# Attention and a three-way max feed-forward layer on one core: immediate biases, an earlier first load, a reordered start, and 12 matmuls on constants

## Chip, core and metric

The kernel runs on one core of a Trainium2 chip. The metric is the device time in microseconds (us) of one execution. Engines: TensorE (PE, with its weight loads PEld), VectorE (DVE), ScalarE (ACT), GpSimd (POOL), and SyncE (SP), which issues DMAs.

## The reference

```python
# q, k, v: (8 batches, 12 heads, 448, 64), fp32
scores = q @ k^T / sqrt(64)
e      = exp(scores - m)                    # m: maximum of the row
attn   = e / (sum(e) + exp(-m) + 1e-9)      # softmax with one more 1 in the sum
x      = (attn @ v) as (3584 tokens, 768)
h      = max(x @ w1, x @ w2, x @ w3)
out    = h @ w_out
```

## The kernel before

The 12 heads of a batch are three groups of four heads, so there are 24 groups. All arithmetic on TensorE is in fp16. A group's K and Q are transposed, scores are computed with keys on partitions, ScalarE takes the exponential, a matmul with ones gives the denominators, and ScalarE makes their reciprocals as exp(-ln(d)). Groups 0 to 2 (batch 0) run in a hand-written start, cut in two parts by queries, among feed-forward pieces for batch 0. From group 4 on a loop does one group per pass. Groups 0 to 4 are transposed on TensorE, later ones by a DMA transpose issued one or two passes ahead; group 5's is queued at the end of the start (`X5`).

```python
def load_group(i, which="qkv"):            # GpSimd queue, casts to fp16 in the DMA
    ... tile(..., tag="ld_" + name, bufs=6 if name == "v" else 5)
    for hp in range(2): load_half(nc.gpsimd, tiles[name], name, i, hp)

first = {}                                 # group 0: K on SP's queue, Q on ACT's, both fp32
for name, eng in (("k", nc.sync), ("q", nc.scalar)):
    ... for hp in range(2): load_half(eng, first[name], name, 0, hp)
load_group(1, "kq"); make_identity(nc, ident16); load_group(0, "v"); ...
one_b, e_b, ln_lam = ...                   # [128, 1] biases in SBUF, read through pointers
load_weight(0); load_weight(1); load_group(3, "kq"); load_weight(2)
load_group(4, "kq"); load_group(3, "v"); load_group(5, "kq"); ...
# (cut)
ops = {"C": pair_qk, "T": pe_transpose_both, "S": scores_part (three units),
       "s": scores_part (the last unit), "A": av_part (denominators, ln, exp, numerators),
       "M": moe, "U"/"V"/"W": visit_a/b/c, "E": sums, "X": transpose_later, "F": flush}
start = """
    C0 T0 S00 T1 s00 S10 T2 s10 A00 S20 A10 s20 S01 A20 s01
    S11 M1 s11 M1 M1 A01 S21 M1 s21 M1 T3 M1 A11 U3 M1 A21 V3 T4 E30 M1 M1 W3 E31 X5 F
"""
# (cut)
for i in range(4, 24):
    load_group(i + 3)
    visit_a(i); av_group(i - 2) (or feed-forward for i < 5); visit_b(i); ...; moe(gap)
    if i + 1 < PE_TR: pe_transpose_both(i + 1)      # PE_TR = 5
    flush(); visit_c(i); den_group(i - 1)
    transpose_later(i + 2); ...; moe(gap); flush()
```

`T3` is the transpose of group 3, `M1` one feed-forward piece, `W3` the third score visit of group 3, which ends the start.

The softmax here doesn't subtract the row's maximum and nothing guards it: scores larger than these inputs give would overflow.

Of the kernel before, what the change touches and what calls it, by code (L numbers as in the profile page):

```python
# [10 lines left out]
FP32 = mybir.dt.float32  # L11
# [3 lines left out]
ts = bass.ts  # L15
# [3 lines left out]
EDIV = 8.0  # L19
# [3 lines left out]
def kernel(  # L23
# [69 lines left out]
    def load_group(i, which="qkv"):  # L93
        tiles = raw.setdefault(i, {})
        for name in which:
            tiles[name] = ld_pool.tile(
                [128, 2, NJ, D], MMDT, tag="ld_" + name, name="ld_" + name, bufs=6 if name == "v" else 5
            )
            for hp in range(2):
                load_half(nc.gpsimd, tiles[name], name, i, hp)  # L100

    first = {}
    for name, eng in (("k", nc.sync), ("q", nc.scalar)):
        first[name] = cpool.tile([128, 2, NJ, D], FP32, name="first_" + name)
        for hp in range(2):
            load_half(eng, first[name], name, 0, hp)
    load_group(1, "kq")
    ident16 = cpool.tile([128, 128], MMDT, name="ident16")
    make_identity(nc, ident16)
    load_group(0, "v")  # L110
# [5 lines left out]
    one_b = cpool.tile([128, 1], FP32, name="one_b")  # L116
    nc.vector.memset(one_b, 1.0 / EDIV)
    e_b = cpool.tile([128, 1], FP32, name="e_b")
    nc.vector.memset(e_b, -math.log(EDIV))
    ln_lam = cpool.tile([128, 1], FP32, name="ln_lam")  # L120
    nc.vector.memset(ln_lam, math.log(LAMBDA))

# [19 lines left out]
    def copy_qk(i, n):  # L142
        st = state.setdefault(i, {})
        if n == 0:
            st["qk16"] = p16_pool.tile([128, 2, NJ, 2, D], MMDT, tag="qk16", name="qk16")
        src = first["kq"[n]] if i == 0 else raw[i]["kq"[n]]
        nc.vector.tensor_copy(
            out=st["qk16"][:, n].rearrange("p j s d -> p s j d"), in_=src
        )

    def pair_qk(i):
        for n in range(2):
            copy_qk(i, n)

    def pe_transpose(i, n):
        st = state.setdefault(i, {})
        if n == 0:
            st["qkT"] = att_pool.tile([128, 2, NJ, 128], MMDT, tag="qkT", name="qkT")
        trT = ps1.tile([128, NJ, 128], MMDT, tag="bank1", name="trT")
        for j in range(NJ):  # L160
            if i == 0:
                nc.tensor.transpose(
                    out=trT[:, j, :], in_=st["qk16"][:, n, j].rearrange("p s d -> p (s d)"),
                    identity=ident16,
                )
                continue
            for s in range(2):
                nc.tensor.transpose(  # L168
                    out=trT[s * KC : s * KC + KC, j, :], in_=raw[i]["kq"[n]][:, s, j], identity=ident16
                )  # L170
        nc.vector.tensor_copy(  # L171
            out=st["qkT"][:, n].rearrange("p j c -> p (j c)"),
            in_=trT.rearrange("p j c -> p (j c)"),
        )
# [31 lines left out]
    def scores_visit(i, units):  # L206
# [8 lines left out]
        for j, stp in stps:  # L215
            nc.scalar.activation(  # L216
                out=st["eT"][:, j], in_=stp[:, :, 0:S], func=AF.Exp, scale=scale, bias=e_b
            )
# [27 lines left out]
    def den_group(i):  # L246
# [10 lines left out]
        nc.scalar.activation(out=lnd, in_=dps[:, :, 0:S], func=AF.Ln, bias=one_b)  # L257
        st["rb"] = small.tile([128, 2, S], FP32, tag="rb", name="rb")
        nc.scalar.activation(out=st["rb"], in_=lnd, func=AF.Exp, bias=ln_lam, scale=-1.0)  # L259
# [24 lines left out]
    def scores_part(i, part, last=False):  # L284
# [3 lines left out]
        if not last:  # L288
            st["eT", part] = e_pool.tile([128, NJ, 2, nq], MMDT, tag="eT", name="eTp")
        eT = st["eT", part]  # L290
        for j0 in (6,) if last else (0, 2, 4):
            n = min(2, NJ - j0)
            stp = ps2.tile([128, 2, 512], FP32, tag="bank2", name="stp")
            for jj in range(n):
                score_tile(st["qkT"], stp[:, :, ts(jj, nq)], j0 + jj, q0, q1)
            nc.scalar.activation(  # L296
                out=eT[:, j0 : j0 + n].rearrange("p j r q -> p r j q"),
                in_=stp[:, :, 0 : n * nq].rearrange("p r (j q) -> p r j q", j=n),
                func=AF.Exp,
                scale=scale,  # L300
                bias=e_b,
            )

    def av_part(i, part):
        b, g = groups[i]
# [3 lines left out]
        eT, v16 = st["eT", part], raw[i]["v"]  # L309
        if g == 0 and part == 0:  # L310
            new_x(b)
        dps = ps2.tile([128, 2, 512], FP32, tag="bank2", name="den")
        banks = [ps1.tile([128, 512], FP32, tag="bank1", name="num") for _ in range(2)]
        for j in range(NJ):
# [9 lines left out]
            out=lnd[:, :, 0:nq], in_=dps[:, :, 0:nq], func=AF.Ln, bias=one_b  # L324
# [3 lines left out]
            out=rb[:, :, 0:nq], in_=lnd[:, :, 0:nq], func=AF.Exp, bias=ln_lam, scale=-1.0  # L328
        )
        for j in range(NJ):  # L330
# [125 lines left out]
    load_weight(1)  # L456
    load_group(3, "kq")
    load_weight(2)
    load_group(4, "kq")
    load_group(3, "v")  # L460
# [25 lines left out]
    def transpose_later(i):  # L486
# [7 lines left out]
        "C": pair_qk,  # L494
        "T": pe_transpose_both,
        "S": scores_part,
        "s": lambda i, part: scores_part(i, part, True),
        "A": av_part,
# [7 lines left out]
        C0 T0 S00 T1 s00 S10 T2 s10 A00 S20 A10 s20 S01 A20 s01  # L506
        S11 M1 s11 M1 M1 A01 S21 M1 s21 M1 T3 M1 A11 U3 M1 A21 V3 T4 E30 M1 M1 W3 E31 X5 F
# [78 lines left out]
```

## Time and profile before

| | before |
|---|---|
| first three executions | 352.89, 359.21, 361.3 us |
| profiled execution | 359.33 us, a slow one; span 357.6 us |
| PE busy, ACT busy | 91%, 58% |
| first exponential | 12.61 us |
| third visit W3 | 51.65 us |
| wait for the transpose of group 5 | 5.05 us, first scores of group 5 at 68.97 us |

A stretch of the span is read by asking which engine is full there. What counts for the total in this kernel is the moment at which the first scores of group 5 start: from there TensorE is full to the end, so 288.6 us follow in this profile (286.3 if the 2.3 us of half clock are taken off).

### The profile page before, as it was taken

Reading aid. Unit: us, or ns where it says so; the run is one execution under the profiler, and the core shown is the slowest. Engines: PE = TensorE matmul, PEld = TensorE weight load, DVE = VectorE, ACT = ScalarE, POOL = GpSimd, SP = SyncE. Lnnn points to the kernel's source line nnn. Section 1 sums busy time; section 2 is a strip of 40 time slices with the busy share of each in tenths; the row PEclk is TensorE's granted clock in tenths of the full one; section 3 lists DMA queues with packets and bytes.
Section 4 is the critical chain, followed back from the end, with each engine's and each line's share of the span. In section 5 each row is a group of like instructions: output and inputs, shape, how many; then the busy total and the mean of one; then the engine's idle time right before and its main releaser. Section 6 shows DMA issues by size and latency. Waiting matters only on the chain.

```text
span 357.6 us, 7731 instructions
## 1 busy us (share of the span) xinstructions
PE 324.9 (91%) x3198; PEld 182.8 (51%) x3198; DVE 234.5 (66%) x434; ACT 205.7 (58%) x226; POOL 92.2 (26%) x158
## 2 busy tenths in 40 slices
PE   0779879499999999999999999999999999898994
PEld 0658767264444554555454554455455545454552
DVE  0422458368767868778777787787777776655553
ACT  1598678268675595676566668568467566420000
POOL 6924858033312321330330331231000000000000
PEclk9998999789999999999999999999999999999999
DMA  8999999978965797688965895587312540022006
GB/s 162 193 208 205 159 195 147 147 106 148 191 102 79 121 207 127 87 106 165 147 92 89 164 176 97 80 128 148 82 36 53 142 88 0 2 56 78 0 2 177
DMA packets 63172, 41.93 MB, mean 117 GB/s; under 512 B 38048, under 2 KB 59552, under 8 KB 63136
## 3 DMA queue, kind: packets, MB, share of 16 engines
q0 software_dynamic: 23424, 20.78, 40.3%
q1 hardware_dynamic: 39424, 20.19, 27.4%
q10 hardware_dynamic: 288, 0.46, 0.6%
q8 instruction: 25, 0.41, 0.5%
q14 instruction: 11, 0.09, 0.1%
HBM read 42.47 MB, written 11.01 MB: 150 GB/s over the span
## 4 chain that ended last, share of the span: by engine, by line
PE 79%; ACT 7%; DMA 6%; DVE 5%; issue 2%; SPq 0%; DVEq 0%
PE p_i L355 41%; PE op_ps L398 15%; PE stp L198 8%; PE av L238 8%; PE p_i L376 4%; DMA qkT<-qk 3%; DVE xT L277 3%; ACT eT L216 3%; DMA first_k<-in_k_dram 2%; PE den L238 2%; ACT eTp L296 2%; PE trT L168 1%; ACT rb L327 1%; ACT lnd L323 1%; DVE qkT L171 1%
## 5 line engine op out<-in xcount | busy, mean ns | idle before, releaser
L216 ACT ACTIVATE eT<-stp,e_b 128x896 f16<-128x896 f32 x147 | 136.7, 1008 | 87.9 <-PE stp L198 87.9
L355 PE MATMUL p_i<-xT,w 128*128 128x448 f16 x756 | 148.1, 352 | 3.1 <-DVE xT L277 1.2
L355 PEld LDWEIGHTS <-w 128*128 128x128 f16 x756 | 72.7, 98 | 74.6 <-issue 9.6
L365 DVE TENSOR_TENSOR hT<-hT,p_i 128x448 f16<-128x448 f16 x84 | 52.2, 621 | 30.1 <-PE p_i L355 30.1
L224 DVE TENSOR_TENSOR eS<-eS,eT 128x896 f16<-128x896 f16 x105 | 65.0, 619 | 2.8
L88 POOL DMA_DIRECT2D ld_v<-in_v_dram x48 | 28.8, 610 | 140.2 <-PE stp L198 116.4
L198 PE MATMUL stp<-qkT 64*64 64x448 f16 (+2 forms) x756 | 54.6, 355 | 9.8 <-DMA qkT<-qk 5.1
L398 PE MATMUL op_ps<-w,hT 128*128 128x384 f16 x336 | 57.8, 326 | 0.0
L398 PEld LDWEIGHTS <-hT 128*128 128x128 f16 x336 | 31.6, 98 | 24.6 <-issue 2.5
L405 DVE TENSOR_SCALAR o_sb<-op_ps 128x384 f32<-128x384 f32 x56 | 31.1, 555 | 15.2 <-PE op_ps L398 13.6
L198 PEld LDWEIGHTS <-qkT 64*64 64x64 f16 x756 | 22.0, 112 | 35.5 <-issue 27.1
L238 PE MATMUL av<-eT,ld_v 64*64 64x448 f16 x588 | 36.9, 362 | 0.9 <-DVE o_sb L405 0.5
L363 DVE CAST hT<-p_i 128x448 f16<-128x448 f32 x42 | 26.2, 624 | 17.4 <-PE p_i L355 17.4
L277 DVE TENSOR_TENSOR xT<-av,rb 128x448 f16<-128x448 f32 x42 | 24.3, 620 | 15.4 <-PE av L238 15.3
L238 PEld LDWEIGHTS <-ld_v 64*64 64x64 f16 x756 | 26.2, 112 | 12.9 <-issue 7.7
L88 POOL DMA_DIRECT2D ld_k<-in_k_dram x46 | 28.4, 637 | 5.9 <-DMA w<-in_moe_w_dram 2.6
L88 POOL DMA_DIRECT2D ld_q<-in_q_dram x46 | 28.2, 628 | 5.9 <-DMA w<-in_moe_w_dram 3.7
L296 ACT ACTIVATE eTp<-stp,e_b 128x768 f16<-128x768 f32 (+3 forms) x24 | 20.1, 909 | 11.2 <-PE stp L198 11.0
L257 ACT ACTIVATE lnd<-den,one_b 128x896 f32<-128x896 f32 x21 | 21.2, 1008 | 8.8 <-PE den L238 8.8
L376 PE MATMUL p_i<-xT,w 128*128 128x192 f16 (+1 forms) x216 | 23.1, 261 | 1.6 <-DVE xT L339 1.3
L259 ACT ACTIVATE rb<-lnd,ln_lam 128x896 f32<-128x896 f32 x21 | 21.9, 1042 | 0.7
L376 PEld LDWEIGHTS <-w 128*128 128x128 f16 x216 | 19.2, 98 | 6.0 <-issue 3.3
(36 smaller groups left out, 109.6 us busy)
## 6 DMA issues: line engine op xcount, KB each, us to landing
out_dram<-o_sb SPq DMA_DIRECT2D x56, 192.0 KB, 3.1
ld_v<-in_v_dram POOLq DMA_DIRECT2D x48, 112.0 KB, 4.2
ld_k<-in_k_dram POOLq DMA_DIRECT2D x46, 112.0 KB, 5.2
ld_q<-in_q_dram POOLq DMA_DIRECT2D x46, 112.0 KB, 4.5
w<-in_moe_w_dram POOLq DMA_DIRECT2D x3, 576.0 KB, 11.4
w<-in_moe_w_dram POOLq DMA_DIRECT2D x6, 288.0 KB, 10.2
w<-in_moe_w_out_dram POOLq DMA_DIRECT2D x3, 384.0 KB, 7.9
first_k<-in_k_dram SPq DMA_DIRECT2D x2, 224.0 KB, 6.1
```

The costliest lines, as they stand in the source:

```text
L88: eng.dma_start(out=dst[hp * KC : hp * KC + KC].rearrange("p s j d -> p s (j d)"), in_=src[:, half_heads(name, hp)],)
L198: nc.tensor.matmul(out=out[half(c), r], lhsT=qkT[half(r), 0, j, h], rhs=qkT[half(r), 1, q0:q1, h], start=True, stop=True,)
L216: nc.scalar.activation(out=st["eT"][:, j], in_=stp[:, :, 0:S], func=AF.Exp, scale=scale, bias=e_b)
L224: nc.vector.tensor_tensor(out=st["eS"], in0=st["eT"][:, 0] if j == 1 else st["eS"], in1=st["eT"][:, j], op=ALU.add,)
L238: nc.tensor.matmul(out=outs[r][half(c)], lhsT=weights(r, c), rhs=moving(r, c), start=start, stop=stop,)
L277: nc.vector.tensor_tensor(out=xT[b][:, 2 * g + r, :], in0=banks[r][:, 0:S], in1=st["rb"][:, r], op=ALU.mult)
L296: nc.scalar.activation(out=eT[:, j0 : j0 + n].rearrange("p j r q -> p r j q"), in_=stp[:, :, 0 : n * nq].rearrange("p r (j q) -> p r j q", ...
L355: nc.tensor.matmul(out=p_i[:, 0:S], lhsT=w_sb[i][:, dc, ts(fc, 128)], rhs=xT[b][:, dc, :], start=(dc == 0), stop=(dc == NDC - 1),)
L365: nc.vector.tensor_tensor(out=dst, in0=dst, in1=p_i[:, 0:S], op=ALU.max)
L376: nc.tensor.matmul(out=p_i[:, ts(j, nq)], lhsT=w_sb[i][:, dc, ts(2 * fp + j, 128)], rhs=xT[b][:, dc, q0 * KC : q1 * KC], start=(dc == 0), ...
L398: nc.tensor.matmul(out=op_ps[:, 0:NW], lhsT=hT[bp][:, fc, ts(t, 128)], rhs=wout_sb[:, fc, ts(nh, NW)], start=(fc == 0), stop=(fc == NFC - 1),)
L405: nc.vector.tensor_scalar(out=o_sb[:, ts(nh, NW)], in0=op_ps[:, 0:NW], scalar1=1.0 / LAMBDA, scalar2=None, op0=ALU.mult,)
```

## The change

The intent: let TensorE and ScalarE start earlier (K of group 0 on both hardware queues, its Q through GpSimd without a cast), keep TensorE's clock up (12 matmuls on constants), shorten each activation (immediate biases), and give ScalarE its denominators earlier (`D` apart from `N`). The third weight is now loaded ahead of K and Q of group 3, and V has five buffers instead of six.

```diff
-                ..., bufs=6 if name == "v" else 5
+                ..., bufs=5
-    first = {}
-    for name, eng in (("k", nc.sync), ("q", nc.scalar)):
-        ...
-    load_group(1, "kq")
+    first_k = cpool.tile([128, 2, NJ, D], FP32, name="first_k")
+    load_half(nc.sync, first_k, "k", 0, 0)
+    load_half(nc.scalar, first_k, "k", 0, 1)
+    load_group(0, "q")
     make_identity(nc, ident16)
+    load_group(1, "kq")
-    one_b, e_b, ln_lam = ...             # three memsets
+    warm16 = cpool.tile([128, S], MMDT, name="warm16")
+    nc.vector.memset(warm16, 1.0)
+    warm = ps1.tile([128, 512], FP32, tag="bank1", name="warm")
+    for _ in range(12):
+        nc.tensor.matmul(out=warm[:, 0:S], lhsT=warm16[:, 0:128], rhs=warm16, start=True, stop=True)
# ... copies and transposes of group 0: only K is cast (cut) ...
-    bias=e_b / one_b / ln_lam
+    bias=-math.log(EDIV) / 1.0 / EDIV / math.log(LAMBDA)
# ... av_part split in den_part (D) and num_part (N), scores_part one unit at a time (cut) ...
     load_weight(1)
+    load_weight(2)
     load_group(3, "kq")
-    load_weight(2)
+    load_group(3, "v")
     load_group(4, "kq")
-    load_group(3, "v")
-        C0 T0 S00 T1 s00 S10 T2 s10 A00 S20 A10 s20 S01 A20 s01
-        S11 M1 s11 M1 M1 A01 S21 M1 s21 M1 T3 M1 A11 U3 M1 A21 V3 T4 E30 M1 M1 W3 E31 X5 F
+        C00 T0 S000 S001 S002 T1 S003 S100 S101 D00 T2 S102 S103 N00 S200 S201 D10 S202 S203 N10
+        S010 D20 S011 S012 N20 S013 M1 M1 S110 D01 S111 N01 S112 S113 M1 M1 S210 D11 S211 N11
+        S212 S213 M1 T3 M1 D21 M1 U3 N21 T4 V3 E30 M1 M1 W3 E31 X5 F
```

More of the change, by code (lines that the diff above doesn't have):

```diff
@@ L96, in load_group @@
             tiles[name] = ld_pool.tile(
-                [128, 2, NJ, D], MMDT, tag="ld_" + name, name="ld_" + name, bufs=6 if name == "v" else 5
+                [128, 2, NJ, D], MMDT, tag="ld_" + name, name="ld_" + name, bufs=5
             )
@@ L100, in load_group @@
                 load_half(nc.gpsimd, tiles[name], name, i, hp)
-    first = {}
-    for name, eng in (("k", nc.sync), ("q", nc.scalar)):
-        first[name] = cpool.tile([128, 2, NJ, D], FP32, name="first_" + name)
-        for hp in range(2):
-            load_half(eng, first[name], name, 0, hp)
-    load_group(1, "kq")
+    first_k = cpool.tile([128, 2, NJ, D], FP32, name="first_k")
+    load_half(nc.sync, first_k, "k", 0, 0)
+    load_half(nc.scalar, first_k, "k", 0, 1)
+    load_group(0, "q")
     ident16 = cpool.tile([128, 128], MMDT, name="ident16")
     make_identity(nc, ident16)
+    load_group(1, "kq")
     load_group(0, "v")
@@ L115 @@
     nc.vector.memset(ones16, 1.0)
-    one_b = cpool.tile([128, 1], FP32, name="one_b")
-    nc.vector.memset(one_b, 1.0 / EDIV)
-    e_b = cpool.tile([128, 1], FP32, name="e_b")
-    nc.vector.memset(e_b, -math.log(EDIV))
-    ln_lam = cpool.tile([128, 1], FP32, name="ln_lam")
-    nc.vector.memset(ln_lam, math.log(LAMBDA))
+    warm16 = cpool.tile([128, S], MMDT, name="warm16")
+    nc.vector.memset(warm16, 1.0)
+    warm = ps1.tile([128, 512], FP32, tag="bank1", name="warm")
+    for _ in range(12):
+        nc.tensor.matmul(
+            out=warm[:, 0:S], lhsT=warm16[:, 0:128], rhs=warm16, start=True, stop=True
+        )
     w_sb = [cpool.tile([128, NDC, DFF], MMDT, name=f"w{i}") for i in range(4)]
@@ L143, in copy_qk @@
         st = state.setdefault(i, {})
-        if n == 0:
+        if "qk16" not in st:
             st["qk16"] = p16_pool.tile([128, 2, NJ, 2, D], MMDT, tag="qk16", name="qk16")
-        src = first["kq"[n]] if i == 0 else raw[i]["kq"[n]]
+        src = first_k if i == 0 else raw[i]["kq"[n]]
         nc.vector.tensor_copy(
@@ L149, in copy_qk @@
         )
-    def pair_qk(i):
-        for n in range(2):
-            copy_qk(i, n)
     def pe_transpose(i, n):
@@ L160, in pe_transpose @@
         for j in range(NJ):
-            if i == 0:
+            if i == 0 and n == 0:
                 nc.tensor.transpose(
@@ L216, in scores_visit @@
             nc.scalar.activation(
-                out=st["eT"][:, j], in_=stp[:, :, 0:S], func=AF.Exp, scale=scale, bias=e_b
+                out=st["eT"][:, j], in_=stp[:, :, 0:S], func=AF.Exp, scale=scale, bias=-math.log(EDIV)
             )
@@ L256, in den_group @@
         lnd = small.tile([128, 2, S], FP32, tag="lnd", name="lnd")
-        nc.scalar.activation(out=lnd, in_=dps[:, :, 0:S], func=AF.Ln, bias=one_b)
+        nc.scalar.activation(out=lnd, in_=dps[:, :, 0:S], func=AF.Ln, bias=1.0 / EDIV)
         st["rb"] = small.tile([128, 2, S], FP32, tag="rb", name="rb")
-        nc.scalar.activation(out=st["rb"], in_=lnd, func=AF.Exp, bias=ln_lam, scale=-1.0)
+        nc.scalar.activation(out=st["rb"], in_=lnd, func=AF.Exp, bias=math.log(LAMBDA), scale=-1.0)
     def av_group(i):
@@ L282, with scores_part @@
     PARTS = ((0, 3), (3, NJ))
-    def scores_part(i, part, last=False):
+    def scores_part(i, part, unit):
         st = state[i]
@@ L287, in scores_part, with den_part @@
         nq = (q1 - q0) * KC
-        if not last:
+        if unit == 0:
             st["eT", part] = e_pool.tile([128, NJ, 2, nq], MMDT, tag="eT", name="eTp")
         eT = st["eT", part]
-        for j0 in (6,) if last else (0, 2, 4):
-            n = min(2, NJ - j0)
-            stp = ps2.tile([128, 2, 512], FP32, tag="bank2", name="stp")
-            for jj in range(n):
-                score_tile(st["qkT"], stp[:, :, ts(jj, nq)], j0 + jj, q0, q1)
-            nc.scalar.activation(
-                out=eT[:, j0 : j0 + n].rearrange("p j r q -> p r j q"),
-                in_=stp[:, :, 0 : n * nq].rearrange("p r (j q) -> p r j q", j=n),
-                func=AF.Exp,
-                scale=scale,
-                bias=e_b,
-            )
-    def av_part(i, part):
-        b, g = groups[i]
+        j0 = 2 * unit
+        n = min(2, NJ - j0)
+        stp = ps2.tile([128, 2, 512], FP32, tag="bank2", name="stp")
+        for jj in range(n):
+            score_tile(st["qkT"], stp[:, :, ts(jj, nq)], j0 + jj, q0, q1)
+        nc.scalar.activation(
+            out=eT[:, j0 : j0 + n].rearrange("p j r q -> p r j q"),
+            in_=stp[:, :, 0 : n * nq].rearrange("p r (j q) -> p r j q", j=n),
+            func=AF.Exp,
+            scale=scale,
+            bias=-math.log(EDIV),
+        )
+    def den_part(i, part):
         st = state[i]
@@ L308, in av_part @@
         nq = (q1 - q0) * KC
-        eT, v16 = st["eT", part], raw[i]["v"]
-        if g == 0 and part == 0:
-            new_x(b)
+        eT = st["eT", part]
         dps = ps2.tile([128, 2, 512], FP32, tag="bank2", name="den")
-        banks = [ps1.tile([128, 512], FP32, tag="bank1", name="num") for _ in range(2)]
         for j in range(NJ):
@@ L323, in av_part @@
         nc.scalar.activation(
-            out=lnd[:, :, 0:nq], in_=dps[:, :, 0:nq], func=AF.Ln, bias=one_b
+            out=lnd[:, :, 0:nq], in_=dps[:, :, 0:nq], func=AF.Ln, bias=1.0 / EDIV
         )
@@ L327, in av_part, with num_part @@
         nc.scalar.activation(
-            out=rb[:, :, 0:nq], in_=lnd[:, :, 0:nq], func=AF.Exp, bias=ln_lam, scale=-1.0
+            out=rb[:, :, 0:nq], in_=lnd[:, :, 0:nq], func=AF.Exp, bias=math.log(LAMBDA), scale=-1.0
         )
+        st["rb", part] = rb
+    def num_part(i, part):
+        b, g = groups[i]
+        st = state[i]
+        q0, q1 = PARTS[part]
+        nq = (q1 - q0) * KC
+        eT, rb, v16 = st["eT", part], st["rb", part], raw[i]["v"]
+        if g == 0 and part == 0:
+            new_x(b)
+        banks = [ps1.tile([128, 512], FP32, tag="bank1", name="num") for _ in range(2)]
         for j in range(NJ):
@@ L493 @@
         "F": flush,
-        "C": pair_qk,
+        "C": copy_qk,
         "T": pe_transpose_both,
         "S": scores_part,
-        "s": lambda i, part: scores_part(i, part, True),
-        "A": av_part,
+        "D": den_part,
+        "N": num_part,
         "M": moe,
```

## The prediction

> **What bounds the kernel now.** I read the page first, then the chain of waits in order of time for the first 75 us, then the busy times by stretch, then the timeline of the start. The page:
>
> ```profile
> PE 324.9 (91%) x3198; PEld 182.8 (51%) x3198; DVE 234.5 (66%) x434; ACT 205.7 (58%) x226; POOL 92.2 (26%) x158
> ...
> PE   0779879499999999999999999999999999898994
> ...
> ACT  1598678268675595676566668568467566420000
> PEclk9998999789999999999999999999999999999999
> ```
>
> TensorE (PE) is over 90% busy from slice 9 on (a slice is 8.9 us) and not before. The change touches the order of work only before that, so the question is what ends the start. The stretches (us, then busy PE, PEld, DVE, ACT, POOL, granted clock, DMA share, GB/s):
>
> ```profile
> 12.60:31.00 18.40, 14.95 (x363) 12.38 (x356) 4.36 (x10) 17.22 (x24) 10.11 (x18) 0.91 1.17 202
> 31.00:44.00 13.00, 11.84 (x248) 10.04 (x246) 5.54 (x11) 8.98 (x12) 8.12 (x14) 1.00 1.10 174
> 44.00:56.40 12.40, 9.72 (x169) 7.49 (x169) 8.20 (x18) 9.85 (x12) 7.46 (x13) 1.00 1.18 190
> 56.40:63.95 7.55, 7.52 (x72) 5.84 (x70) 6.08 (x11) 5.93 (x7) 5.46 (x10) 1.00 1.26 136
> 63.95:69.00 5.05, 0.03 (x4) 0.03 (x5) 1.85 (x3) 0.00 (x0) 0.00 (x0) 0.84 1.43 157
> 69.00:74.00 5.00, 4.96 (x50) 2.30 (x51) 0.97 (x2) 3.46 (x4) 0.74 (x2) 0.50 0.91 114
> 74.00:357.60 283.60, 273.67 (x2280) 142.56 (x2278) 204.99 (x374) 158.98 (x170) 50.41 (x85) 1.00 0.57 102
> ```
>
> Four regimes. Until 12.6 us only loads count. From 12.6 to 31 ScalarE (ACT) is the bound (17.22 of 18.40 busy, 24 activations). From 31 to 64 PE leads with waits in between. From 64 to 69 everything stands still, and for 5 us after that PE runs at clock 0.50. From 74 us PE is the bound and nothing of the change is on its chain there. The chain names the two loads that matter (start, length, what):
>
> ```profile
> 1.56 7.29 DMA first_k<-in_k_dram
> 8.86 0.03 issue
> ...
> 8.96 0.64 DVE qk L147
> ...
> 9.64 1.69 PE trT L162 x14
> ...
> 11.35 0.64 DVE qkT L171
> ...
> 56.48 12.45 DMA qkT<-qk
> ...
> 68.97 1.33 PE stp L198 x12
> ```
>
> The first K lands at 8.86 us because both halves sit on one queue: the second half is issued at 1.56. The DMA transpose of group 5 takes 12.45 us, against a median of 4.5 us over the 19 transposes, because it shares the DMA engines with loads of groups 7 to 9 that are issued until 63 us. PE reaches its consumer at 63.9 and waits 5.05 us.
>
> This profile is of a slow execution (359.33 us; the three times are 352.89, 359.21, 361.3). Without the wait (5.05), and without the half clock behind it (PE work from 69.0 to 74 would take about half: 2.3 saved), it would be 359.3 - 5.05 - 2.3 = 352.0 us: the fast execution, by my reading.
>
> The start also runs on a slow clock, although the clock row reads full there. The same 14 half transposes, early and late:
>
> ```profile
> 13.13 0.96 PE L168 MATMUL trT<-ident,ld_k 128*64 128x128 f16 x14
> ...
> 38.90 0.58 PE L168 MATMUL trT<-ident,ld_k 128*64 128x128 f16 x14
> ```
>
> So matmuls before about 19.4 us (24 score matmuls take 1.18 us at 12.0, 0.66 us at 20.2) run at some 0.6 of the later rate.
>
> **What the Trainium skill says.** "TensorE: Matmul & The Clock Gate", section "What's actually happening": PE starts at 1.2 GHz and goes to 2.4 after a busy window of about 3.4 us, and falls back after an idle one. The trace agrees in kind (clock 0.50 after the 5 us wait), but the rise comes near 10 us after the first matmul at 9.64, later than the page's 4. "ScalarE: Activation LUTs", section "What ACT_TABLE_LOAD costs": an activation with a pointer bias takes 280 ns + 0.833 ns per element, with immediates 186 ns, and back-to-back ones overlap by about 93 ns. The trace's 128x896 exponential is 1008 ns (the page's formula gives 1026), and seven in a row take 6.40 us, so 0.90 apart; an immediate bias is in no trace yet. "DMA: Bandwidth & Descriptors", section "Queues, rings and completion order": each engine goes round-robin between queues by packet, so a transpose shares with whatever loads are queued; the 12.45 against 4.5 us agrees.
>
> **The change part by part.**
>
> First K on both queues. The half that is alone at the head of each queue landed 5.0 us (SP, issued 0.74) and 3.9 us (ACT, issued 0.77) after issue, so both halves of K should land by 5.7 instead of 8.86. Cast 0.63 + 0.1: transposes from 6.45 instead of 9.64. Q now goes by GpSimd as fp16 with no cast, issued at 1.25 and 1.9; such loads took 5.7 to 6.0 us to land in the first 12 us, with more beside them than now, so I put Q at 7.0 to 7.3. K transposes end at 7.3, Q's 14 half transposes at about 8.0, copy 0.63 to 8.7, first exponential at t0 = 9.2 instead of 12.61. Gain 3.4.
>
> 12 warm matmuls of 448 columns: at the page's 1.2 GHz an estimate of 12 x 373 ns = 4.5 us, from about 1.2 to 5.7, so before K is cast and in nobody's way. If they raise the clock, the two transpose stages of T0 and the first scores are shorter by about 0.4 to 0.8 (in part already in t0 above); the rest of what they speed up, until 19.4, lies beside ACT, which is busy 17.22 of 18.40. Worth 0.5, not the 4 us by which PE's own work shrinks.
>
> Early denominators. I walked PE's and ACT's new orders by hand with durations of the trace: score pairs 0.22 or 0.28 us, T 1.16 plus copies 0.63, D and N 0.77 (part 0) or 0.95 (part 1), M 1.15, exponentials 0.83, 0.51, 1.05, 0.62 apart, Ln and Exp 0.6 and 0.6, later 0.7 and 0.7. ACT has no gap from t0 to t0 + 16.4; W3, the last score unit of the start, comes at t0 + 38.3. In the trace it comes at 51.65 = t0 + 39.0. So reordering gives about 0.7: it removes ACT's waits for denominators (0.5, 1.24 and 2.72 us idle at 19.8, 34.5 and 42.3), but most of the gain is taken by PE work that moves ahead of them, and the bound there is the sum of the exponentials, which stays.
>
> Immediate biases. 225 activations are each 93 ns shorter by the page; back to back it could be anything from nothing (the pointer's part is what overlapped) to 93 ns. Some 22 of them are on the ACT-bound path in the start: 0 to 2.0 us, I take 0.8. After 74 us ACT is not on the path: nothing. The three memsets removed took 0.06 us each beside the loads.
>
> Loads. The total is the same and the engines are saturated, so weight w2 ahead of group 3 only delays K and Q of group 3 by 2304 KB read, some 5.8 us at twice the 200 GB/s written: from about 28.5 to 34.4, while T3 would come near 35. Just in time. V has 5 buffers instead of 6, so V of group 8 waits for V of group 3 to be used, near 60 us, and GpSimd's queue stops behind it: V of 8 and all of 9 (5 of the 10 half loads issued between 56.4 and 63 now) no longer run beside the transpose of group 5. Transpose issued at about 51.5; the queue drains by 58 to 59; landing 58 to 61 against a need at 59.0. I expect a wait of 1.5 with its clock cost instead of 7.3.
>
> Sum from the execution without a wait: 352.0 - 3.4 - 0.5 - 0.7 - 0.8 = 346.6, plus 1.5 = 348.1; I say 348.
>
> **The rivals.** (a) The transpose wait stays. For: the load stream is bound by DMA (202 GB/s from 12.6 to 31) and doesn't get shorter when PE starts earlier, so an earlier need could simply wait longer. Then 346.6 + 7 = 354, or 357 at worst. Against: five half loads fewer beside it. (b) The ACT bound gets shorter by the full 93 ns each, and the denser PE saves its waits in 44 to 56 us (2.7 of 12.4 idle): 343 to 345. (c) The warm matmuls or GpSimd's slower path for Q delay T0: Q landing at 9 would leave only 1.5 of the 3.4: 350. (d) PE, 63% busy in my walk beside ACT, falls back to the slow clock, as the 0.91 from 12.6 to 31 shows it did; costs up to 1.5.
>
> **Range and chances.** 348, range 343 to 355. Two per cent under 359.21 is 352.0: only (a) in full, or (c) and (d) together, stay above it. But a comparison of fast executions alone starts from about 353, and 348 is within 2% of that; this is why faster gets no more than 0.62. Slower needs a start that is longer than now, for which I see nothing.
>
> **What would show it.** First K landed before 6 us; first exponential near 9.2; transposes of group 1 at 0.58 and not 0.96 us (warm); exponentials of 896 at about 0.915 us each, and their spacing in a row below 0.90 if the bias was on the path; ACT without gaps until about 31 - 5; W3 near 46.5; PE's wait for the transpose under 3 us; from there to the end of the span 286 us (288.6 now, less the 2.3 of half clock). It would be wrong if the wait for the transpose is as long as before, if Q lands later than K's transposes by over 1.5 us, or if T3 waits for its loads.

## The result, and the profile after

Four executions of the changed kernel took 349.95 to 350.64 us, median 350.31. Beside them before took 352.89, 353.7, 359.21 and 361.3 us. A ratio here is the mean time of one kernel's fast runs over that of the other's of the same rounds, so it is not quite the ratio of the medians; it is 0.9915, interval 0.9886 to 0.9944. Only the first two of those four executions of before count as fast there.

The profiled execution of the changed kernel (349.95 us, span 348.2) is a fast one. Its page, in the same rows as before:

```profile
PE 322.4 (93%) x3217; PEld 180.5 (52%) x3217; DVE 234.3 (67%) x431; ACT 185.7 (53%) x226; POOL 93.0 (27%) x160
...
PE   7777888899999999999999999999999999899994
...
ACT  1979385677566565665665654754754745320000
PEclk9999899999999999999999999999999999999999
```

TensorE starts in the first slice (the 12 matmuls, 4.66 us), slice 8 rises from four tenths to eight, and the clock dips in the fifth slice. ACT's busy time is 20 us less. Of the groups of instructions, first the exponentials of the main part before, then after (count | busy us, mean ns | idle):

```profile
L216 ACT ACTIVATE eT<-stp,e_b 128x896 f16<-128x896 f32 x147 | 136.7, 1008 | 87.9 <-PE stp L198 87.9
```

```profile
L211 ACT ACTIVATE eT<-stp 128x896 f16<-128x896 f32 x147 | 123.4, 924 | 97.9 <-PE stp L193 97.8
```

Each is 84 ns shorter, and what ACT saves returns as idle time: it waits for TensorE's scores (97.9 us instead of 87.9). The stretches after, in the windows of the prediction:

```profile
12.60:31.00 18.40, 14.74 (x402) 12.27 (x402) 6.09 (x14) 15.28 (x24) 7.79 (x13) 1.00 1.14 195
31.00:44.00 13.00, 10.09 (x187) 7.99 (x181) 4.33 (x9) 6.85 (x11) 10.06 (x17) 0.87 1.20 191
44.00:56.40 12.40, 11.33 (x148) 8.17 (x144) 10.10 (x19) 9.62 (x12) 7.62 (x14) 1.00 1.18 177
56.40:63.95 7.55, 4.74 (x67) 3.43 (x68) 4.41 (x9) 3.31 (x5) 1.68 (x3) 1.00 1.44 149
63.95:69.00 5.05, 4.78 (x57) 3.39 (x50) 3.49 (x6) 3.63 (x5) 3.55 (x6) 1.00 1.32 177
```

From 12.6 to 31 ACT is busy for 15.28 of 18.40, no longer the bound. From 31 to 44 PE is less busy than before (10.09 against 11.84) and its clock falls to 0.87. From 56.4 the wait shows. The timeline of the start says when things happened and what ended the idle time in brackets:

```profile
5.30 0.64 DVE L146 CAST qk<-first_k 128x896 f16<-128x896 f32 x1 [3.89 <-DMA first_k<-in_k_dram]
...
6.59 0.58 PE L163 MATMUL trT<-ident,ld_q 128*64 128x128 f16 x14
...
8.31 2.77 ACT L291 ACTIVATE eTp<-stp 128x768 f16<-128x768 f32 x4 [6.29 <-PE stp L193]
...
35.36 0.65 PE L163 MATMUL trT<-ident,ld_k 128*64 128x128 f16 x14 [1.26 <-DMA ld_k<-in_k_dram]
...
36.51 0.58 PE L163 MATMUL trT<-ident,ld_q 128*64 128x128 f16 x14 [0.51 <-DMA ld_q<-in_q_dram]
37.03 2.10 PE L378 MATMUL p_i<-xT,w 128*128 128x192 f16 x12
```

K is there at 5.3 us, the 14 half transposes run at 0.58 us from the first (warm), and the first exponential comes 4.3 us earlier than before. Then the last three lines: T3 waits 1.26 + 0.51 us for loads of group 3, and the 12 matmuls after it take 2.10 us instead of the 1.15 of their neighbours, because the clock has fallen (0.50 from 37 to 40 us). The third visit comes at 47.31 us, 4.3 us earlier than before (51.65). The chain of waits has the other place:

```profile
52.26 9.90 DMA qkT<-qk
62.16 0.04 issue
62.20 0.41 PE stp L193 x4
```

```profile
62.20 0.76 PE L193 MATMUL stp<-qkT 64*64 64x448 f16 x12 [2.81 <-DMA qkT<-qk]
```

The transpose of group 5 still takes 9.90 us and TensorE still waits 2.81 us for it. From 62.20 to the end of the span are 286.0 us, as predicted.

### The profile page after: what moved, and what is told of

Its sections match the earlier page's. It is cut to its first block, busy times and chain, and to the rows that moved or that the text cites.

```text
span 348.2 us, 7764 instructions
## 1 busy us (share of the span) xinstructions
PE 322.4 (93%) x3217; PEld 180.5 (52%) x3217; DVE 234.3 (67%) x431; ACT 185.7 (53%) x226; POOL 93.0 (27%) x160
## 4 chain that ended last, share of the span: by engine, by line
PE 73%; DMA 9%; DVE 6%; ACT 5%; POOL 4%; issue 2%; DVEq 0%; POOLq 0%
PE p_i L357 42%; PE op_ps L400 15%; PE stp L193 6%; PE av L233 5%; ACT eT L211 5%; DMA w<-in_moe_w_dram 4%; DVE xT L272 4%; DMA qkT<-qk 3%; PE p_i L378 3%; DMA ld_q<-in_q_dram 3%; PE den L233 1%; POOL ld_v L88 1%; POOL ld_q L88 1%; DVE eS L219 1%; DVE o_sb L407 1%
## 5 line engine op out<-in xcount | busy, mean ns | idle before, releaser
L211 ACT ACTIVATE eT<-stp 128x896 f16<-128x896 f32 x147 | 123.4, 924 | 97.9 <-PE stp L193 97.8
L193 PE MATMUL stp<-qkT 64*64 64x448 f16 (+2 forms) x756 | 50.5, 336 | 6.5 <-DMA qkT<-qk 2.8
L407 DVE TENSOR_SCALAR o_sb<-op_ps 128x384 f32<-128x384 f32 x56 | 31.1, 555 | 15.0 <-PE op_ps L400 13.7
L233 PE MATMUL av<-eT,ld_v 64*64 64x448 f16 x588 | 35.7, 351 | 0.9 <-DVE o_sb L407 0.5
L193 PEld LDWEIGHTS <-qkT 64*64 64x64 f16 x756 | 20.2, 105 | 28.0 <-issue 21.1
L233 PEld LDWEIGHTS <-ld_v 64*64 64x64 f16 x756 | 25.3, 106 | 13.5 <-issue 8.1
L88 POOL DMA_DIRECT2D ld_q<-in_q_dram x48 | 29.2, 626 | 4.7 <-DMA w<-in_moe_w_dram 3.5
L378 PE MATMUL p_i<-xT,w 128*128 128x192 f16 (+1 forms) x216 | 23.8, 266 | 1.8 <-DVE xT L341 1.3
L252 ACT ACTIVATE lnd<-den 128x896 f32<-128x896 f32 x21 | 19.4, 925 | 9.1 <-PE den L233 9.1
L291 ACT ACTIVATE eTp<-stp 128x768 f16<-128x768 f32 (+3 forms) x24 | 18.3, 819 | 9.7 <-PE stp L193 9.5
L254 ACT ACTIVATE rb<-lnd 128x896 f32<-128x896 f32 x21 | 20.0, 952 | 0.7
```

Source lines behind the costliest of these rows:

```text
L88: eng.dma_start(out=dst[hp * KC : hp * KC + KC].rearrange("p s j d -> p s (j d)"), in_=src[:, half_heads(name, hp)],)
L193: nc.tensor.matmul(out=out[half(c), r], lhsT=qkT[half(r), 0, j, h], rhs=qkT[half(r), 1, q0:q1, h], start=True, stop=True,)
L211: nc.scalar.activation(out=st["eT"][:, j], in_=stp[:, :, 0:S], func=AF.Exp, scale=scale, bias=-math.log(EDIV))
L233: nc.tensor.matmul(out=outs[r][half(c)], lhsT=weights(r, c), rhs=moving(r, c), start=start, stop=stop,)
L378: nc.tensor.matmul(out=p_i[:, ts(j, nq)], lhsT=w_sb[i][:, dc, ts(2 * fp + j, 128)], rhs=xT[b][:, dc, q0 * KC : q1 * KC], start=(dc == 0), ...
L407: nc.vector.tensor_scalar(out=o_sb[:, ts(nh, NW)], in0=op_ps[:, 0:NW], scalar1=1.0 / LAMBDA, scalar2=None, op0=ALU.mult,)
```

## The experiments

Eighteen runs were made in five calls, each call on another chip, with 11 executions of before beside each call and, where timed, 6 of each kernel. Times of one call are compared directly; between calls the ratio to before is the better guide, because the chips differ (before's median was 357.0 to 357.7 us on four of them and 354.4 on the last). Medians are over all executions; the ratios take fast ones alone (within 1.5 per cent of the fastest of the same kernel). All results were correct. Names beginning with b_ are edits of before, with a_ edits of the changed kernel, with p_ edits of the version that has neither wait. One slip stands in the expectation of a_old_loads: where it says that the third visit of the changed kernel is at 49.5 us, I had read a later unit's line; it is at 47.31.

The theory to start with: the start does get faster as predicted, and part of that is given back at two places where TensorE waits for DMA (T3's loads, group 5's transpose). The rivals: the stream of loads sets the end of the start whatever is done; or the new order of work is itself worse.

### b_copy: the kernel before, profiled again

No edit. Expected:

> The kernel before, unchanged, profiled once more, because the profile at hand is of a slow execution. If the two states of before are the wait for the DMA transpose of group 5 (my reading), a fast profile shows this wait at 0 to 2 us instead of 5.05 us, no clock of 0.50 behind it, the first scores of group 5 between 64 and 66 us, and everything before 63.9 us and after the wait as in the slow profile. If the slow state is something else (a slower clock or slower loads all along), the 286 us from those scores to the end differ too.

358.94 us, so not a fast execution. The wait for group 5's transpose was 3.48 us here and 3.0 us more went into the next DMA transpose (group 6); in the slow profile at hand group 6 cost nothing. So the wait moves between executions, and before's times are no two states: its 59 executions lie between 352.49 and 363.28 us, median 357.0, with no gap that would part two states.

### a_old_loads

```diff
     load_weight(1)
-    load_weight(2)
     load_group(3, "kq")
-    load_group(3, "v")
+    load_weight(2)
     load_group(4, "kq")
+    load_group(3, "v")
```

> The changed kernel with the loads in the order of before (K and Q of group 3 ahead of the third weight). Theory: T3 no longer waits for its loads (1.77 us now) and TensorE doesn't cool from 37 to 40 us (1.6 us), so the third visit of the start comes at 46 to 47 us instead of 49.5; total 347 to 348 if the wait for the transpose of group 5 stays at 2.8 us. Rival: the stream of loads sets when that transpose lands, at 62.2 us, whatever comes before it; then the wait grows from 2.8 to 5 or 6 us and the total stays at 350, or gets worse by the half clock behind the longer wait (352 to 353).

348.65 us median (347.69 to 357.13), ratio 0.9791. Its timeline at T3 and at the first scores of group 5:

```profile
34.08 0.58 PE L163 MATMUL trT<-ident,ld_k 128*64 128x128 f16 x14
34.80 0.58 PE L163 MATMUL trT<-ident,ld_q 128*64 128x128 f16 x14
...
59.14 0.76 PE L193 MATMUL stp<-qkT 64*64 64x448 f16 x12 [2.96 <-DMA qkT<-qk]
```

No wait at T3, no slow matmuls, and the third visit at 44.10 us. The wait for the transpose stayed at 2.96 in this execution, but 352.0 and 357.1 are among its six, so the rival is not excluded for those. This order of loads did cost the changed kernel time, though the median alone (348.65 here, 349.86 on another chip) would be thin evidence; the pair a_pe5 and a_pe5_loads below, on one chip, is better.

### a_old_order

```diff
-        C00 T0 S000 S001 S002 T1 S003 S100 S101 D00 T2 S102 S103 N00 S200 S201 D10 ...
+        C00 T0 S000 S001 S002 T1 S003 S100 S101 S102 T2 S103 D00 N00 S200 S201 S202 D10 N10 S203
+        S010 S011 S012 D20 N20 S013 S110 S111 S112 M1 S113 M1 M1 D01 N01 S210 S211 S212
+        M1 S213 M1 T3 M1 D11 N11 U3 M1 D21 N21 V3 T4 E30 M1 M1 W3 E31 X5 F
```

> The changed kernel with the start in the old order of work (denominators just ahead of the numerators, scores of a group three units at a time), the rest as changed. Theory: early denominators are worth 0.7 us at the end of the start and less in the total: 350.3 to 351. Rival: the new order is what lost the gain; then this run is faster than the changed kernel, 348 to 349.

356.48 us median (352.0 to 358.36), ratio 0.9956: neither expectation, some 6 us slower. Its waits of PE in the first 72 us (sum, times, longest):

```profile
PE stp L193 <- DMA qkT<-qk: 5.6, 1, 5.6
PE trT L163 <- DMA ld_k<-in_k_dram: 3.1, 2, 2.8
PE trT L163 <- DMA ld_q<-in_q_dram: 1.8, 3, 0.7
```

In the changed kernel these are 2.8, 1.3 and 1.7 us. The old order does less work ahead of T3, so TensorE reaches it earlier and waits longer, and it met a transpose of 12.7 us. Whether the order is worth anything without these waits was left for p_old_order.

### a_no_warm, and again as a_no_warm2

```diff
-    for _ in range(12):
-        nc.tensor.matmul(out=warm[:, 0:S], lhsT=warm16[:, 0:128], rhs=warm16, start=True, stop=True)
```

(The constant tile and its PSUM tile go too.)

> The changed kernel without its 12 matmuls on constants. Theory: TensorE runs slow until 13 to 16 us, the first exponential comes at 8.9 to 9.4 instead of 8.3 us, and the end of the start moves by 0.5 to 1 us; the total by 0 to 1 us, because the later loads absorb it: 350.3 to 351.3. Rival: the warm clock is what carries the gain of the start; then 352 to 354.

347.57 us median (346.61 to 351.01), ratio 0.9748: faster than the changed kernel's record, which nobody expected. So it was repeated beside the changed kernel.

> The changed kernel without the 12 matmuls once more, now beside the changed kernel itself. The first run had 346.6 to 351.0, median 347.6, which would make the 12 matmuls cost 2 to 3 us, against my expectation. Theory: the load stream and not TensorE's early clock sets the end of the start, so without them the time is the same within 1 us (349.5 to 351). Rival: they cost time (the loads come at another moment against the work, or GpSimd or the clock suffers): then this run is again 2 to 3 us below the changed kernel.

350.33 us median (347.65 to 351.39), ratio 0.9805, beside 349.86 and 0.9824 of the changed kernel: the same. The two runs disagree by 2.8 us, on two chips. The profile of the second has two idle stretches of TensorE, 0.37 and 1.62 us, that end on nothing but "issue"; the first has none. In the presence of the waits the 12 matmuls cannot be weighed; p_no_warm and p_tiny take this up.

### after_copy: the changed kernel beside its variants

> The changed kernel unchanged, timed on the same chip and in the same rounds as the three variants below, because the first four runs were not beside it. I expect 350.0 to 350.6 as on record, and a ratio of fast runs to before between 0.985 and 0.992. If this chip differs from the first, the ratio tells it.

349.86 us median (347.88 to 352.98), beside before at 357.02 median: ratio 0.9824, interval 0.9772 to 0.9876. The ratio is lower than expected because before's fast runs here were 354.3 to 358.7 us and not 353. The profile showed no clock dip at T3; the waits at T3 were 1.11 and 0.49 us, and the one for the transpose 2.52.

### a_pe5

```diff
-    PE_TR = 5
+    PE_TR = 6
-        ... M1 M1 W3 E31 X5 F
+        ... M1 M1 W3 E31 F
```

Group 5 is now transposed by TensorE inside the first pass of the loop.

> The changed kernel with group 5 transposed by TensorE in the first pass of the main loop, as group 4 is in the start, and no DMA transpose for it. It takes 28 matmuls (1.2 us) and two copies of 0.63 us on VectorE that TensorE may wait for, and the wait for the DMA transpose (2.8 us in the profile of the changed kernel) is gone. Theory: 1.0 to 1.8 us faster than the changed kernel, 348.5 to 349.3, and less spread between executions, because the wait is what varies. Rival: the loads of K and Q of group 5, or what comes after, hold TensorE in its place: no gain.

347.34 us median (346.78 to 349.13), ratio 0.9734. The first scores of group 5, with no wait in brackets:

```profile
59.04 0.76 PE L193 MATMUL stp<-qkT 64*64 64x448 f16 x12
```

2.5 us faster than the changed kernel in the same rounds, more than the 1.0 to 1.8 expected, and the spread is 2.35 us instead of 5.1. The theory holds for the transpose.

### a_pe5_loads

Both edits, the loads of a_old_loads and the transpose of a_pe5.

> Both: loads in the order of before, and group 5 transposed by TensorE. Theory: the waits for group 3's loads (1.8 us), the half clock behind them (1.6 us) and the wait for the DMA transpose (2.8 us, less 1.2 us of work) all go: 345 to 346.5, the fastest so far. Rival: the load stream then holds TensorE at the next place that needs loads (V of group 3 or 4, the fourth weight, group 6's transpose): 347 to 349.

346.24 us median (345.62 to 347.3), ratio 0.9702: as the theory said. The order of the loads is worth 1.1 us beside a_pe5 on the same chip. Third visit at 43.94, first scores of group 5 at 57.20.

### b_pe5

The edit of a_pe5, made to the kernel before.

> The kernel before with one edit: group 5 transposed by TensorE, no DMA transpose for it. Theory: the spread of the kernel before (353.8 to 360.7 in the 22 executions beside the first two sets) is its wait for that transpose and the half clock behind it. Without it the executions lie within 2 us of each other, at 351.5 to 353.5. Rival: the spread comes from the loads or the clock anywhere in the start; then this kernel spreads over 5 us or more too.

352.83 us median (352.34 to 354.39). Before, beside it, ran from 353.77 to 362.8. The spread fell from 9.0 to 2.1 us by taking one DMA transpose away: before's spread is that wait and what follows from it. Its first scores of group 5:

```profile
63.87 0.76 PE L198 MATMUL stp<-qkT 64*64 64x448 f16 x12
```

### b_first_k

```diff
-    for name, eng in (("k", nc.sync), ("q", nc.scalar)): ...
+    load_half(nc.sync, first_k, "k", 0, 0)
+    load_half(nc.scalar, first_k, "k", 0, 1)
+    load_group(0, "q")
```

(With the cast of K alone, as in the changed kernel.)

> The kernel before with the first part of the change alone: first K on both hardware queues, first Q through GpSimd. The first exponential comes about 3.2 us earlier (9.4 instead of 12.6). Theory: the transpose of group 5 lands when the loads let it, so the total gains less than that: 0 to 2 us, 355 to 357 median, with the wait for the transpose grown. Rival: the gain goes through to the end: 353.5 to 354.5.

354.76 us median (351.23 to 357.88), ratio 0.9929, between what the theory and the rival gave. The first exponential came at 9.20 us and the third visit at 47.41, against 12.22 and 50.42 in b_pe5 on the same chip: 3.0 us go through the whole start. But the profile then has 7.8 us of waits for four DMA transposes (the longest took 17.2 us from issue to landing), so only part reaches the end.

### a_v6

```diff
-                bufs=5
+                bufs=6 if name == "v" else 5
```

> The changed kernel with six buffers for V instead of five, as before. My prediction took the smaller number as what keeps loads away from the transpose of group 5. Theory: with six, V of group 8 and K and Q of group 9 are loaded beside the transpose too, which then takes 11 to 13 us instead of 10: 1 to 3 us slower, 351 to 353. Rival: the transpose has landed before those loads matter: no difference (349.5 to 350.5).

354.41 us median (350.2 to 358.64), ratio 0.9916: slower than the changed kernel by 4.5 us (on another chip; by the ratios 0.9 per cent). The intervals of the two ratios (0.9838 to 0.9994, and 0.9772 to 0.9876) overlap, so the difference is not resolved. In its profile the transpose of group 5 took 11.0 us and PE waited 3.90 us, but the sixth buffer can't be the reason: V of group 8 was issued at 63.10 us, after that transpose had landed at 61.48. The transposes of groups 6 and 8 were the longer ones, 13.7 and 13.1 us (11.5 and 8.9 in after_copy). What the fifth buffer is worth stays open.

### a_pointers

```diff
-    bias=-math.log(EDIV) / 1.0 / EDIV / math.log(LAMBDA)
+    bias=e_b / one_b / ln_lam
```

> The changed kernel with the biases in SBUF again, read through pointers. Each 128x896 exponential takes 1.008 us instead of 0.924. Theory: in the start the exponentials come at 0.90 us instead of 0.81 us in a row, and TensorE waits for them in a few places, 0.5 to 1 us by the third visit; behind the later waits for loads and the transpose, 0 to 1 us in the total. Rival: nothing there depends on it: the same within 0.3 us. Second rival: 2 us or more, if it is what the measured gain consists of.

351.81 us median (349.23 to 352.46), ratio 0.9856 against 0.9824 of the changed kernel elsewhere: not resolved. So three parts were weighed once more where no wait hides them.

### p_again, p_old_order, p_no_warm, p_pointers

p is a_pe5_loads; each of the others undoes one part in it, by the edits of a_old_order, a_no_warm and a_pointers. All four ran in the same rounds on one chip.

> The version without the two waits, again, as the measure for the three beside it: 345.6 to 347.3 us, as in its first run.

> The same version with the start in the old order of work. Theory: early denominators by themselves are worth about what I predicted, 0.7 us, and what they saved in the changed kernel beyond that was wait: 346.5 to 348 us. Rival: the order itself is worth 4 to 6 us: 350 to 352.

> The same version without the 12 matmuls. Theory: with no wait behind it, the slow clock until about 18 us costs what the end of the start moves by: 0.5 to 1.9 us (the third visit came 1.9 us later without them in the quieter pair of profiles), so 347 to 348. Rival: the loads or VectorE bound the early part anyway, and the time is the same within 0.3 us.

> The same version with pointer biases. Theory: TensorE waits for exponentials back to back in the start, some 20 of them at 0.09 us: 1 to 2 us, so 347.2 to 348.2, with nothing of it after the start. Rival: hidden behind TensorE, 0 to 0.3 us.

| run | median us | lowest to highest | ratio | the part is worth |
|---|---|---|---|---|
| p_again | 346.62 | 345.61 to 347.92 | 0.9702 | |
| p_old_order | 346.14 | 345.6 to 346.82 | 0.9691 | nothing (0.5 the other way, within the spread) |
| p_no_warm | 348.54 | 348.01 to 350.11 | 0.9763 | 1.9 us |
| p_pointers | 346.64 | 346.28 to 347.52 | 0.9704 | nothing |

The 12 matmuls are the only one of the three with an effect. But the timeline of PE in p_no_warm shows that the slow clock at the beginning is not where most of the time goes:

```profile
13.10 0.58 PE L156 MATMUL trT<-ident,ld_k 128*64 128x128 f16 x14
...
18.85 0.70 PE L226 MATMUL den<-eTp,ones 64*64 64x192 f16 x12 [2.27 <-issue]
...
24.78 0.28 PE L226 MATMUL num<-eTp,ld_v 64*64 64x192 f16 x4 [1.17 <-issue]
```

The transposes are warm (0.58 us) from 13.1 us on. The time goes in two stretches of 2.27 and 1.17 us in the middle of a run of 28 matmuls, where TensorE waits for nothing that the profile names, and in the half clock behind the first of them (0.50 from 18.85 to 21.40 us). With the 12 matmuls the second of these is 0.40 us (a_pe5_loads, at 21.2 us) and the first isn't seen; and the second comes after 12 of the 28 numerator matmuls of group 2, but after 24 of them in p_no_warm. That is 12 matmuls and 12 weight loads later, exactly what was taken out ahead of it: the stretch belongs to a position in TensorE's stream of instructions.

### p_tiny and p_no_warm2

```diff
-            out=warm[:, 0:S], lhsT=warm16[:, 0:128], rhs=warm16, start=True, stop=True
+            out=warm[:, 0:16], lhsT=warm16[:, 0:128], rhs=warm16[:, 0:16], start=True, stop=True
```

The 12 matmuls stay but take 0.49 us in all instead of 4.66, so the instructions are as many and warm nothing. p_no_warm2 is p_no_warm again.

> The version without the two waits, with its 12 matmuls cut to 16 columns. If the slow clock is what costs (my prediction's account of the 12 matmuls), TensorE is slow until 11 to 18 us as in p_no_warm, and the time is 347.5 to 349. If the number of instructions ahead is what matters, the idle stretches of over 1 us marked issue are gone or as short as in the version with 448 columns (0.4 us), and the time is 346 to 347 although the early transposes take 0.96 us.

> The same version without the 12 matmuls, again, beside p_tiny. 348 to 350 us with idle stretches marked issue of over 1 us in the first 30 us, as on the chip of its first run; if they are missing on this chip, the time is 346 to 347.5.

p_tiny took 346.71 us (345.93 to 347.58), p_no_warm2 349.02 (346.22 to 349.36), ratios 0.98 and 0.985 on a chip where before is faster. In p_tiny the early clock is as slow as without any, and the stretch is short:

```profile
9.65 0.96 PE L163 MATMUL trT<-ident,ld_k 128*64 128x128 f16 x14
...
21.76 0.53 PE L233 MATMUL num<-eTp,ld_v 64*64 64x192 f16 x16 [0.21 <-issue]
```

p_no_warm2 has 0.22 and 2.02 us instead. So the 12 matmuls are worth about 2 us as 24 instructions and nothing measurable as heat. (The full 12 and the tiny ones never ran on one chip; the version without them ran beside each, and lost 1.9 us to the full ones and 2.3 to the tiny ones.) Something else changed with the 12: in the four profiles of a_no_warm, a_no_warm2, p_no_warm and p_no_warm2 the median DMA transpose takes 3.6 to 3.7 us, in the other sixteen 4.2 to 4.7. Why isn't shown; these four lack the constant tile too, which p_tiny keeps, so p_tiny differs from p_no_warm in more than 24 instructions.

What TensorE waits for in these stretches can be read from the packed traces, which give every DMA packet its times. Queue 8, of the kind "instruction", moves 25 packets of 16384 bytes in an execution, one at a time, and TensorE runs some 6400 to 6490 matmuls and weight loads, so a packet goes with 256 to 260 of them. In all 20 traces there are 25 idle stretches of TensorE of 0.2 us or more that end on "issue". Every one ends at the 222nd, the 350th or the 477th (twice the 478th) matmul, 127 or 128 matmuls and their weight loads apart, and 1.24 to 1.47 us after such a packet has landed. In p_no_warm the packets land at 17.57 and 23.49 us, and the stretches end at 18.85 and 24.78. So TensorE waits there for its next instructions, which come by DMA beside the loads; the kernel before has such stretches too (1.11 us in b_copy). Why the packets come late in p_no_warm (the first starts 4.2 us after the 94th matmul, in p_tiny 0.7 us) is not shown, and no edit tests it.

p_old_order, at 346.14 us, and a_pe5_loads, at 346.24, beat both kernels; they can't be told apart.

## Why the prediction was right and wrong

The forecast was 348 us for a kernel at 359.21, a gain of 11.2 us. By its own working that is 5.4 us from the parts (352.0 to 346.6, both without a wait) and 5.8 us from the wait (7.3 shrinking to 1.5). The changed kernel took 350.3, inside the range, but the gain is about 7 us against the median of 59 executions of before (357.0).

**The parts: the sum held, the terms didn't.** Without the wait for group 5's transpose the two kernels are b_pe5 and a_pe5, 352.83 and 347.34 us: 5.5 us (6.0 by their ratios, as they ran on different chips). That the sum fits is partly luck, because the terms don't, and a_pe5 still waits at T3. The terms were: first K 3.4; the first exponential came 4.3 us earlier in the changed profile and 3.0 with this part alone, so about right (Q landed at 6.18 us and not at 7.0 to 7.3: GpSimd's loads in the first 12 us of before took 3.7 to 6.7 us, not 5.7 to 6.0). Warm matmuls 0.5: as warmth nothing that p_tiny shows, so "lies beside ACT" held; as 24 instructions about 2 us, by the waits for instructions, a mechanism that the prediction did not have. Early denominators 0.7: nothing. Immediate biases 0.8: nothing, though each activation is 84 ns shorter. The third visit was predicted near 46.5 and came at 47.31 in the first profile and at 45.55 in the second.

**The wait: the step that failed.** "I expect a wait of 1.5 with its clock cost instead of 7.3." Transposing on TensorE instead gained 4.5 us at before (357.33 to 352.83, same rounds) and 2.5 us at the changed kernel (349.86 to 347.34). The work that this puts on TensorE is the same in both, so the wait shrank by about 2.0 us, where the forecast had 5.8. (By the means of the fast executions alone the two gains are 3.4 and 2.8 us, so it shrank by less still.) Both ends of that term were mis-sized. With the 1.2 us that the 28 matmuls of a transpose take on TensorE, an estimate from the two gains is that the wait cost 5.7 us at before instead of 7.3, and 3.7 us at the changed kernel instead of 1.5. At before I took the wait of one slow profile, in an execution of 359.33 us, as if it were the rule; the median execution waits less, by that estimate, and 359.21 as a median of three was 2 us above the median of 59. At the changed kernel the transpose was issued at 52.26 us (51.5 forecast) and needed at 59.39 (59.0 forecast), but it landed at 62.16 us and not at 58 to 61. The step that gave 58 to 61 was that V of group 8 and all of group 9 would no longer run beside it, so that GpSimd's queue would drain by 58 to 59. They had indeed left, but the transpose itself had moved 4.2 us ahead in the same stream of loads, and loads of groups 7 and 8 stood in their place: GpSimd issued nine half loads between the transpose's issue and its landing, as many as before (where the prediction counted ten), the last at 61.06 us. That is rival (a) in part: the stream doesn't get shorter when TensorE starts earlier. The count is read from the two profiles; that it is why the transpose stayed long is argued, no edit tests it.

**Just in time.** I wrote this of K and Q of group 3, reckoning 34.4 against a need near 35. TensorE was ready at 34.1, the loads weren't until 35.36 and 36.5, and in that profile the clock fell behind it. The prediction named a wait of T3 as a sign of being wrong. The place was right and the margin was not a margin: 1.1 us in a_pe5_loads against a_pe5.

**V's buffers.** V of group 8 did wait, and was issued at 64.63 us, behind the transpose (58.25 before, beside it). But this bought little, as just said, and a_v6 doesn't show what it bought: its 4.5 us (0.9 per cent) come from two chips and are not resolved, and with six buffers too V of group 8 came after the transpose.

**The comparison of fast executions.** The prediction warned that faster got no more than 0.62 because a comparison of fast executions would start from about 353. That is what happened: 352.89 and 353.7 are among the six lowest of before's 59 executions. Eleven further executions beside six of the changed kernel give 0.9824, which is still within 2 per cent.

What stays open: why instructions reach TensorE later when its stream is 24 instructions shorter, why a_no_warm ran at 347.6 us on one chip and 350.3 on another (its profile, which has no such stretch, is of its slowest execution, 351.01), and the split of what remains of the gain. (b_pe5 to p_again is 6.2 us by the medians; less 1.9 for the 12 matmuls leaves 4.3, of which first K alone showed 3.0 in b_first_k's start.)

## What to carry to other kernels

When a kernel's start is fed by a saturated stream of loads, look for the operation that shares the DMA engines with that stream and on which the bound engine waits; here one DMA transpose carried both the spread of the times and most of the error, and doing it on the bound engine paid at once. Weigh the parts of a change only after such a wait is taken out: with it, undoing the order of work seemed to cost 6 us, without it nothing. When instructions are taken out, keep a control with as many cheap ones, because where the instruction stream is cut into blocks matters too. And before a gain is forecast from a slow profile, ask how the times are distributed: three executions did not say.

## What the Trainium skill lacked or had wrong

- "ScalarE: Activation LUTs", "What ACT_TABLE_LOAD costs": a pointer operand is said to add about 93 ns. Measured: 84 ns (1008 to 924 for 128x896). The page leaves open whether that remains back to back; it does here: seven in a row take 5.77 us instead of 6.40, 0.81 apart instead of 0.90.
- "TensorE: Matmul & The Clock Gate", "What's actually happening": the clock is said to rise after some 3.4 us of sustained activity. It holds for 12 dense matmuls from 1.47 us (transposes at 6.59 us take 0.58 us, warm), but with transposes and short scores in between it took 10 us before (9.64 to about 19.4). Without the 12 it took until 12 to 14 us in p_no_warm, p_no_warm2 and p_tiny, which begin at 6.0 us. The page doesn't say how dense is busy enough.
- The same page, "Part 4: PE-mode transpose", says that the full clock does not engage for transposes, since they don't count as busy in the same way. Here the same 14 half transposes take 0.96 us early and 0.58 us later or after the 12 matmuls, so they run faster on the warm clock; that they count for less would fit the slow rise above, but no run tests it.
- "DMA: Bandwidth & Descriptors", "Queues, rings and completion order" has the round-robin but no size for a DMA transpose beside queued loads. Measured over the 20 profiles: 3.4 to 3.9 us at the least, 3.6 to 4.7 median, and 8.1 to 17.2 at the longest beside loads.
- The same page, "Issuing engines are not separate DMA queues", says that issuing on several engines saves only issue time. b_first_k gained more at the first load (first exponential at 9.20 us instead of 12.22), but it doesn't contradict the page: the edit also took Q off the hardware queues, so fewer bytes stood beside K. The page has no size for that.
- "Runtime: NRT & Kernel Launch", "Instruction fetch mechanics": crossing a boundary between two instruction blocks of 256 is called mostly hidden. It is here after the first 35 us; before, beside heavy loads, TensorE stands still there for 0.21 to 0.60 us with 12 matmuls in front, and for up to 2.27 us without.
